# Computing x by tokens on halves of the array's rows, four chunks in one run, and dividing strip 0's output products at other places

## The chip, the cores and the metric

One core of a Trainium2 chip. The metric is the device time of one execution in microseconds (us). Executions of one kernel agree within about 0.3%. Traces show when each instruction started, to a few nanoseconds.

Engines are named as in the profile: PE is TensorE's matrix products, PEld its weight loads, DVE is VectorE, ACT is ScalarE, POOL is GpSimd, SP the queue that issues most DMAs. PSUM is the buffer in which products land; the kernel uses it as eight banks of 512 columns. A product's weights are its stationary operand; the other operand is streamed past them. The kernel can use the array whole, or as two halves of its columns or of its rows: that is called its tiling here.

## The reference, cut to what matters

```python
# q, k, v: (batch 8, heads 8, tokens 576, dim 64), inputs float32
kv  = einsum('bhsd,bhse->bhde', k, v)                  # 64 x 64 a head
o   = einsum('bhsd,bhde->bhse', q, kv)
x   = o / sqrt(mean(o*o, -1) + 1e-6) * g_norm          # -> (4608 tokens, 512)
out = ((x @ w_a) * (x @ w_b)) @ w_out                  # d_ff = 1536
```

## The kernel before

The second half dominates. Tokens go in nine strips of 512. In a strip, each of 12 column blocks of d_ff is one unit: four products with `w_a` into one PSUM bank, four with `w_b` into another, ACT copies the first (`asb`), DVE multiplies the two (`ab`). Then come four token blocks of 12 output products each. These products are 128x512 and run on the whole array.

The attention of batches 2 to 7 is woven into strips 1 to 6. x is computed by tokens there, in five chunks a batch: q (transposed, two heads in 128 rows) is the stationary operand, and a block-diagonal `kvb` of two heads is streamed. ACT squares, DVE sums, ACT takes the reciprocal root, POOL applies `g_norm`, DVE multiplies, and a transposing DMA puts x into `xt`.

```python
# banks: products a and b rotate over AB, x takes 5 + c % 3, k-by-v sits in 7
AB = (4, 1, 2, 0)
...
def tx(self, c, i):                       # one chunk of 128 tokens
    t0, r = self.rows(c)
    for p in range(NP):                   # 4 pairs of heads
        nc.tensor.matmul(P[:, i, p * 128 : (p + 1) * 128],
                         lhsT=self.qT[:, p, t0 : t0 + 128],
                         rhs=kvb[self.b % 2][:, p, :], start=True, stop=True)
    nc.scalar.activation(sqt[c % 3][r], self.by_head(i)[r], AF.Square)
```

In strip 0 the attention of batch 1 is woven into the output products instead. After token block 0 come six pieces of six products, into one bank only, `O = 3`. The other banks hold attention; bank 6 (`SS`) does so only from the third piece on.

```python
h1, h2 = range(0, FC // 2), range(FC // 2, FC)          # FC = 12
...
pieces = [(1, h1), (1, h2), (2, h1), (2, h2), (3, h1), (3, h2)]
for n, (g, fcs) in enumerate(pieces):
    halves = 0 < n < NP
    o_mm(0, g, O, fcs, halves=halves)                   # 6 products of block g
    if fcs is h2:
        o_out(0, g, O)                                  # DVE or ACT empties bank 3
    if 0 <= n - 2 < NP:
        A.pss(n - 2, SS, halves=halves)                 # sums of squares, banks 6 and 7
        A.pst(n - 2, X[n % 2])
    if 0 <= n - 1 < NP:
        A.x(n - 1, X[(n - 1) % 2], halves)
        A.psq(n - 1, X[(n - 1) % 2])
    if n < NP:
        A.qtr(n, 2)                                     # transposes of q
        A.kv1(n, 2)                                     # k-by-v product, waits for k and v
        A.kv_out(n, P[:, 2, STRIP - D :])
        A.qtr_out(n, 2)
```

## Time and profile before

| | before |
|---|---|
| time, median of the first three runs | 315.73 us |
| span of the profiled run | 313.8 us |
| PE busy | 98% of the span |
| PE's waits on others | 1.2 us and 0.4 us |
| matrix products in the trace | 1935 |

The first lines of the page (busy time, share of the span, instructions), the clock by slices, and the groups of products:

```profile
PE 308.6 (98%) x1935; PEld 149.0 (47%) x1935; DVE 141.5 (45%) x235; ACT 115.9 (37%) x225; POOL 101.2 (32%) x123
...
PEclk9999999999999999999999999999999999999999
...
L321 PE MATMUL P<-xt,wa_t 128*128 128x512 bf16 x432 | 111.9, 380 | 0.0
...
L271 PE MATMUL P<-kvb,qT 128*128 128x128 bf16 x120 | 11.6, 220 | 0.0
```

All waits of PE on other engines, before (who waited, on what: total us, times, longest):

```profile
PE P L407 <- DVE eps_t L424: 1.2, 1, 1.2
PE P L156 <- ACT sq L220: 0.4, 1, 0.4
```

PE is the limit, at full clock. But its ends are modelled (a 128x512 product is shown as 0.38 us long), so a gap of up to 0.17 us can hide in a "busy" PE. The sound reading is the distance from one start to the next. In this trace it is 0.216 us between 128x512 products from 50 us to the end, with few exceptions. The timeline of PE in strip 2 shows the exceptions (start us, us, engine, line, operation, shapes, count):

```profile
87.62 1.03 PE L321 MATMUL P<-xt,wb_t 128*128 128x512 bf16 x4
88.58 0.82 PE L173 MATMUL P<-vtl,ktl 128*64 128x64 bf16 x40
89.33 1.04 PE L321 MATMUL P<-xt,wa_t 128*128 128x512 bf16 x4
90.21 1.03 PE L321 MATMUL P<-xt,wb_t 128*128 128x512 bf16 x4
...
91.93 0.39 PE L271 MATMUL P<-kvb,qT 128*128 128x128 bf16 x4
92.16 1.03 PE L321 MATMUL P<-xt,wb_t 128*128 128x512 bf16 x4
```

Four products with one of the weights take 0.86 us, 4 x 0.216 (those from 89.33 to 90.21, the first after a run, 0.01 longer). A chunk of x (L271) takes 0.223 us (91.933 to 92.156) and costs nothing beyond its own array time. The k-by-v run (L173), which works on halves of the array's columns, is different: from 87.62 to 88.58 is 0.96 us where four products take 0.86. That is the first part of what a change of tiling costs.

In strip 0 the timeline of PE shows the weave of output products (L156 with `wo_t`), transposes (L197) and k-by-v (L173):

```profile
39.23 0.45 PE L197 MATMUL P<-ident,qt 96*64 96x96 bf16 x12
39.79 0.38 PE L173 MATMUL P<-vt,kt 96*64 96x64 bf16 x12
39.97 1.49 PE L156 MATMUL P<-wo_t,ab 128*64 128x512 bf16 x12
...
41.52 0.45 PE L197 MATMUL P<-ident,qt 96*64 96x96 bf16 x12
42.01 0.38 PE L173 MATMUL P<-vt,kt 96*64 96x64 bf16 x12
42.19 1.49 PE L156 MATMUL P<-wo_t,ab 128*64 128x512 bf16 x12
```

Twelve transposes take 0.26 us undisturbed; here 0.56 us pass from 39.23 to 39.79, and 0.49 from 41.52 to 42.01. In both places the k-by-v product starts 0.04 us after its v has landed (39.74 and 41.96 in the trace). These are holes, though the list of waits does not show them. The twelve instructions from 39.97 are the second half of token block 1.

### The profile page before, as it was taken

Reading aid. Unit: us, or ns where it says so; the run is one execution under the profiler, and the core shown is the slowest. Engines: PE = TensorE matmul, PEld = TensorE weight load, DVE = VectorE, ACT = ScalarE, POOL = GpSimd, SP = SyncE. Lnnn points to the kernel's source line nnn. Section 1 sums busy time; section 2 is a strip of 40 time slices with the busy share of each in tenths; the row PEclk is TensorE's granted clock in tenths of the full one; section 3 lists DMA queues with packets and bytes.
Section 4 is the critical chain, followed back from the end, with each engine's and each line's share of the span. In section 5 each row is a group of like instructions: output and inputs, shape, how many; then the busy total and the mean of one; then the engine's idle time right before and its main releaser. Section 6 shows DMA issues by size and latency. Waiting matters only on the chain.

```text
span 313.8 us, 5034 instructions
## 1 busy us (share of the span) xinstructions
PE 308.6 (98%) x1935; PEld 149.0 (47%) x1935; DVE 141.5 (45%) x235; ACT 115.9 (37%) x225; POOL 101.2 (32%) x123
## 2 busy tenths in 40 slices
PE   8999999999999999999999999999999999999995
PEld 3544474454445444544454445544544444444443
DVE  4544335356337703583377123761683134214321
ACT  3643155453246313551464024622651233123310
POOL 8954891282453730139038200320230000000000
PEclk9999999999999999999999999999999999999999
DMA  8999999999799799059988980073022200030002
GB/s 182 197 196 199 201 183 160 229 146 157 172 171 166 103 197 154 2 95 139 207 125 116 169 175 2 17 159 111 1 50 60 102 0 0 36 100 1 0 36 100
DMA packets 94253, 36.19 MB, mean 115 GB/s; under 512 B 64918, under 2 KB 89750, under 8 KB 94230
## 3 DMA queue, kind: packets, MB, share of 16 engines
q0 software_dynamic: 59120, 18.44, 53.8%
q1 hardware_dynamic: 34642, 16.87, 23.3%
q10 hardware_dynamic: 468, 0.57, 0.6%
q8 instruction: 15, 0.25, 0.3%
q14 instruction: 8, 0.07, 0.1%
HBM read 37.78 MB, written 12.98 MB: 162 GB/s over the span
## 4 chain that ended last, share of the span: by engine, by line
PE 86%; DMA 7%; POOL 4%; issue 1%; ACT 0%; POOLq 0%
PE P L321 53%; PE P L156 29%; DMA wb_t<-in_moe_w_b_dram 6%; PE P L271 2%; PE P L173 2%; DMA vt<-in_v_dram 2%; POOL qt L116 1%; POOL wo_t L131 1%; POOL kt L116 1%; POOL vt L116 1%; POOL wa_t L441 0%; POOL wb_t L441 0%; PE P L197 0%; POOL wa_t L127 0%; ACT o_end L619 0%
## 5 line engine op out<-in xcount | busy, mean ns | idle before, releaser
L339 DVE TENSOR_TENSOR ab<-P,asb 128x512 bf16<-128x512 f32 x108 | 74.5, 691 | 103.5 <-PE P L321 87.0
L321 PE MATMUL P<-xt,wa_t 128*128 128x512 bf16 x432 | 111.9, 380 | 0.0
L321 PE MATMUL P<-xt,wb_t 128*128 128x512 bf16 x432 | 111.8, 379 | 0.0
L335 ACT CAST asb<-P 128x512 bf16<-128x512 f32 x108 | 63.0, 585 | 92.4 <-PE P L321 92.4
L156 PE MATMUL P<-wo_t,ab 128*128 128x512 bf16 (+2 forms) x462 | 95.8, 374 | 0.0
L156 PEld LDWEIGHTS <-ab 128*128 128x128 bf16 (+1 forms) x462 | 43.7, 99 | 48.0
L321 PEld LDWEIGHTS <-wa_t 128*128 128x128 bf16 x432 | 41.4, 98 | 47.4 <-issue 0.2
L321 PEld LDWEIGHTS <-wb_t 128*128 128x128 bf16 x432 | 41.5, 98 | 47.0 <-DMA wb_t<-in_moe_w_b_dram 0.2
L294 POOL TENSOR_TENSOR sqt<-rst,g_all 128x512 f32<-128x512 f32 (+1 forms) x24 | 25.0, 1043 | 96.2 <-ACT rst L287 96.2
L392 ACT COPY osb<-P 128x512 f32<-128x512 f32 x17 | 9.9, 585 | 67.5 <-PE P L156 62.2
L394 DVE COPY osb<-P 128x512 f32<-128x512 f32 x18 | 12.4, 691 | 44.0 <-PE P L156 39.5
L139 POOL DMA_DIRECT2D qs<-in_q_dram x12 | 19.8, 1653 | 0.7 <-issue 0.3
L282 DVE TENSOR_REDUCE sst<-sqt 128x8 f32<-128x512 f32 (+1 forms) x24 | 16.3, 680 | 1.9 <-ACT sqt L278 1.4
L303 DVE TENSOR_TENSOR qv<-P,sqt 128x512 bf16<-128x512 f32 (+1 forms) x24 | 16.5, 686 | 0.3
L278 ACT ACTIVATE sqt<-P 128x512 f32<-128x512 f32 (+1 forms) x24 | 14.4, 599 | 4.2 <-PE P L271 4.1
L271 PEld LDWEIGHTS <-qT 128*128 128x128 bf16 x120 | 9.2, 98 | 7.1
L271 PE MATMUL P<-kvb,qT 128*128 128x128 bf16 x120 | 11.6, 220 | 0.0
L287 ACT ACTIVATE rst<-sst,eps_t 128x8 f32<-128x8 f32 (+1 forms) x30 | 9.0, 300 | 4.6 <-DVE sst L282 4.3
L238 DVE SCALAR_TENSOR_TENSOR xt<-P,g_col,rs 128x288 bf16<-128x288 f32 x16 | 7.5, 512 | 5.2 <-ACT rs L228 5.2
L294 POOL TENSOR_TENSOR k_x<-rst,g_all 128x512 f32<-128x512 f32 x6 | 6.3, 1042 | 8.8 <-ACT rst L287 8.8
L131 POOL DMA_DIRECT2D wo_t<-in_moe_w_out_dram x12 | 6.4, 530 | 6.7 <-DMA wb_t<-in_moe_w_b_dram 3.2
L184 ACT CAST kvb<-P 64x64 bf16<-64x64 f32 (+1 forms) x16 | 4.6, 285 | 10.5 <-PE P L173 10.4
(67 smaller groups left out, 123.1 us busy)
## 6 DMA issues: line engine op xcount, KB each, us to landing
out_dram<-osb SPq DMA_DIRECT2D x23, 256.0 KB, 2.1
qs<-in_q_dram POOLq DMA_DIRECT2D x12, 288.0 KB, 6.9
ktl<-in_k_dram POOLq DMA_DIRECT2D x6, 512.0 KB, 8.8
vtl<-in_v_dram POOLq DMA_DIRECT2D x6, 512.0 KB, 11.6
out_dram<-osb SPq DMA_DIRECT2D x13, 128.0 KB, 2.3
wo_t<-in_moe_w_out_dram POOLq DMA_DIRECT2D x12, 128.0 KB, 6.0
wa_t<-in_moe_w_a_dram POOLq DMA_DIRECT2D x5, 256.0 KB, 9.2
wb_t<-in_moe_w_b_dram POOLq DMA_DIRECT2D x5, 256.0 KB, 9.8
```

The source lines that it names most:

```text
L139: nc.gpsimd.dma_start(out=d[:, hs, :], in_=q[b, hs].rearrange("h t d -> t h d"))
L156: nc.tensor.matmul(o[r], lhsT=lhsT[:, r], rhs=rhs, **kw)
L271: nc.tensor.matmul(P[:, i, p * 128 : (p + 1) * 128], lhsT=self.qT[:, p, t0 : t0 + 128], rhs=kvb[self.b % 2][:, p, :], start=True, stop=True,)
L278: nc.scalar.activation(sqt[c % 3][r], self.by_head(i)[r], AF.Square)
L282: nc.vector.reduce_sum(sst[c % 3][r], sqt[c % 3][r], axis=mybir.AxisListType.X)
L294: nc.gpsimd.tensor_mul(sqt[c % 3][r], rst[c % 3][r].unsqueeze(2).to_broadcast([n, H, D]), g_all[r].unsqueeze(1).to_broadcast([n, H, D]),)
L303: nc.vector.tensor_mul(t[r], self.by_head(i)[r], sqt[c % 3][r])
L321: nc.tensor.matmul(self.a if w is wa_t else self.b, lhsT=w[:, kc, self.fc * 128 : (self.fc + 1) * 128], rhs=xt[:, kc, t0 : t0 + STRIP], st ...
L335: nc.scalar.copy(self.t, self.a)
L339: nc.vector.tensor_mul(abt[self.s % 2][self.fc], self.b, self.t)
L392: nc.scalar.copy(t, P[:, i, :])
L394: nc.vector.tensor_copy(t, P[:, i, :])
```

## The change

x is computed by four chunks in one run on halves of the rows: 64x128 weights (one head's q), 64 columns streamed, the lower-row head into banks 4 and 5 and the upper-row head into banks 6 and 7. The last chunk stays whole and comes later, in bank 4. Products a and b rotate over three banks. The k-by-v result is copied whole into `kvs`, and two ACT copies make the block-diagonal `kvb` for the last chunk. Strip 0's 36 output products are divided 8, 6, 6, 6, 5, 5 instead of six times 6.

```diff
+        def tx(self):
+            for c in range(LC):                          # LC = 4
+                t0, _ = self.rows(c)
+                for p in range(NP):
+                    for j, (i, c0) in enumerate(self.place(c)):   # banks 4 or 5, 6 or 7
+                        r = slice(j * D, (j + 1) * D)
+                        nc.tensor.matmul(P[:, i, c0 + p * D : c0 + (p + 1) * D],
+                            lhsT=self.qT[r, p, t0 : t0 + 128],
+                            rhs=self.kvs[r, p, :], start=True, stop=True)
...
-    pieces = [(1, h1), (1, h2), (2, h1), (2, h2), (3, h1), (3, h2)]
-    for n, (g, fcs) in enumerate(pieces):
+    cuts = (12, 20, 26, 32, 38, 43, 48)
+    for n, cut in enumerate(cuts[1:]):
         halves = 0 < n < NP
-        o_mm(0, g, O, fcs, halves=halves)
-        if fcs is h2:
-            o_out(0, g, O)
+        for i in range(cuts[n], cut):
+            g, fc = divmod(i, FC)
+            o_mm(0, g, O, (fc,), halves=halves)
+            if fc == FC - 1:
+                o_out(0, g, O)
...
-    n_ab[0] = 1
+    ab_banks[:] = [0, 1, 2]
```

More of the change, by code (lines that the diff above doesn't have):

```diff
@@ L78 @@
     k32 = k_x[0:EP].rearrange("p (h c d) -> p h c d", h=2, c=EC)
-    sqt = [sb([128, H, D], FP32, f"sqt{i}") for i in range(2)]
-    sqt.append(k_x[:, 0 : H * D].rearrange("p (h d) -> p h d", h=H))
+    sqt = [sb([128, 2, NP, D], FP32, f"sqt{i}") for i in range(2)]
+    sqt.append(k_x[:, 0 : H * D].rearrange("p (j h d) -> p j h d", j=2, h=NP))
     sst = [sb([128, H], FP32, f"sst{i}") for i in range(3)]
@@ L179, in kv, with kv_out @@
                     )
-        def kv_out(self, ps, src, copy=nc.scalar.copy):
+        def kv_out(self, ps, src):
             for j in range(2):
                 r = slice(j * D, (j + 1) * D)
-                copy(kvb[self.b % 2][r, ps, r], src[r])
+                nc.scalar.copy(kvb[self.b % 2][r, ps, r], src[r])
         def kv1(self, p, i):
@@ L263, in rows, with place, by_head, tx_last @@
             return t0, slice(c * 128 - t0, 128)
-        def by_head(self, i):
-            return P[:, i, :].rearrange("t (h d) -> t h d", h=H)
-        def tx(self, c, i):
-            t0, r = self.rows(c)
+        def place(self, c):
+            return tuple((4 + 2 * j + c // 2, c % 2 * (STRIP // 2)) for j in range(2))
+        def by_head(self, c):
+            if c == LC:
+                return P[:, 4, :].rearrange("t (p j d) -> t j p d", j=2, p=NP)
+            (i, c0), (j, _) = self.place(c)
+            o = P[:, i : j + 1 : j - i, c0 : c0 + STRIP // 2]
+            return o.rearrange("t j (p d) -> t j p d", p=NP)
+        def tx(self):
[4 more added lines that the diff above has]
+                        r = slice(j * D, (j + 1) * D)
+                        nc.tensor.matmul(
+                            P[:, i, c0 + p * D : c0 + (p + 1) * D],
+                            lhsT=self.qT[r, p, t0 : t0 + 128],
+                            rhs=self.kvs[r, p, :],
+                            start=True,
+                            stop=True,
+                        )
+        def tx_last(self):
             for p in range(NP):
                 nc.tensor.matmul(
-                    P[:, i, p * 128 : (p + 1) * 128],
-                    lhsT=self.qT[:, p, t0 : t0 + 128],
+                    P[:, 4, p * 128 : (p + 1) * 128],
+                    lhsT=self.qT[:, p, S - 128 : S],
                     rhs=kvb[self.b % 2][:, p, :],
@@ L277, in tx, with tsq @@
                 )
-            nc.scalar.activation(sqt[c % 3][r], self.by_head(i)[r], AF.Square)
+        def tsq(self, c):
+            _, r = self.rows(c)
+            nc.scalar.activation(sqt[c % 3][r], self.by_head(c)[r], AF.Square)
         def tss(self, c):
             _, r = self.rows(c)
-            nc.vector.reduce_sum(sst[c % 3][r], sqt[c % 3][r], axis=mybir.AxisListType.X)
+            nc.vector.reduce_sum(
+                sst[c % 3][r],
+                sqt[c % 3][r].rearrange("t j p d -> t (j p) d"),
+                axis=mybir.AxisListType.X,
+            )
         def trs(self, c):
@@ L294, in trs @@
             nc.gpsimd.tensor_mul(
-                sqt[c % 3][r],
+                sqt[c % 3][r].rearrange("t j p d -> t (j p) d"),
                 rst[c % 3][r].unsqueeze(2).to_broadcast([n, H, D]),
@@ L298, in trs, with txt @@
             )
-        def txt(self, c, i):
+        def txt(self, c):
             t0, r = self.rows(c)
             t = x_tok[c // 3][:, c % 3]
-            nc.vector.tensor_mul(t[r], self.by_head(i)[r], sqt[c % 3][r])
+            nc.vector.tensor_mul(
+                t[r].rearrange("t (p j) d -> t j p d", j=2), self.by_head(c)[r], sqt[c % 3][r]
+            )
             t0 += self.b * S
@@ L343, in rest @@
             self.part_b(kcs)
-    AB = (4, 1, 2, 0)
-    n_ab = [0]
+    ab_banks = [4, 1, 2, 0]
     def ab_bank():
-        n_ab[0] += 1
-        return AB[(n_ab[0] - 1) % len(AB)]
+        ab_banks.append(ab_banks.pop(0))
+        return ab_banks[-1]
     def ffn_ab(s, fc, between=None):
@@ L523 @@
     u3.part_b()
-    n_ab[0] = 0
     for fc in range(4, FC):
@@ L529 @@
     A = Attn(1)
-    h1, h2 = range(0, FC // 2), range(FC // 2, FC)
     nc.sync.dma_start(out=gate_d, in_=vt[1][0:1, H - 1, EC - 1, D - 1 : D])
@@ L570, in slot @@
             xs = tuple(x0 + x for x in (0, 1.5, 2.5, 4, 5))
+        k0, x0 = {1: (5, 6.5), 2: (1, 2.5), 3: (4, 5.5), 4: (0, 0.5), 5: (4, 5.5), 6: (0, 0.5)}[s]
         if n == k0 and s in (1, 2, 3, 5):
@@ L577, in slot @@
             for i, a in enumerate(two):
-                a.kv_out(slice(0, NP), kb[:, i], nc.vector.tensor_copy if i else nc.scalar.copy)
-        for c, x in enumerate(xs):
-            i = 5 + c % 3
-            if n == x:
-                A.tx(c, i)
-            elif n == x + 0.5:
+                (nc.scalar.copy if i else nc.vector.tensor_copy)(a.kvs, kb[:, i])
+        m = n - x0
+        if m == 0:
+            A.tx()
+        if m == 1:
+            A.kv_out(slice(0, NP), A.kvs)
+        if m == 5:
+            A.tx_last()
+        for c in range(LC + 1):
+            if m == 1.5 * c:
+                A.tsq(c)
+            if m == (1, 2, 4, 5, 7)[c]:
                 A.tss(c)
-            elif n == x + 1:
+            if m == (1, 2, 4, 5, 7)[c] + 0.5:
                 A.trs(c)
-            elif n == x + 2.5:
-                A.txt(c, i)
+            if m == (1, 2, 4, 5, 7)[c] + 1.5:
+                A.txt(c)
     for s in range(1, N_STRIP - 1):
```

## The prediction

> **What bounds the kernel now.** TensorE. The page gives PE 98% busy at granted clock 1.0; the list of waits shows PE waiting 1.2 us (start) and 0.4 us. Busy time is modelled, so I read start-to-start distances in the timeline of PE: from 50 us to the end every 128x512 matmul follows the last after 0.216 us; DVE (45%), ACT (37%) and POOL are hidden. Only instructions taken from PE's stream, or gaps in it, are worth time.
>
> **x by tokens, before.** A chunk is 4 whole-array matmuls, 56 ns apart: 0.223 us (timeline: 64.06 to 64.28), no entry cost. 24 of 30 chunks change: 24 x 0.223 = 5.4 us, 1.7% of the time, is all that could be won. Each batch's last chunk is unchanged.
>
> **After.** Per batch 32 matmuls of 64 rows by 128 columns, 64 wide: 16 pairs on halves of the rows, into different banks. The nearest thing in this trace is the k-by-v product (halves of the columns, also 64 wide): 40 matmuls take 0.75 us, a pair each 32 ns. It also prices a change of tiling: the matmul before the run is followed after 0.309 instead of 0.216 us, the first pair takes 20 ns more, the last matmul 0.1 us more: about 0.22 us a run. The Trainium skill, "TensorEngine Tiling (Array Packing)", Key Properties, says that changing the mode drains TensorE; this trace agrees with those 0.22 us.
> Per batch: 0.22 + 16 x 0.032 = 0.74 us against 0.89: 0.95 us saved over six batches. The open term is the pair: its weight loads have 128 columns, not 64. The skill, "TensorE: Matmul & The Clock Gate", Part 3, says loads overlap running matmuls where the row group differs; this trace has no row-only pairs. At 56 ns a pair the part loses 1.35 us; break-even is 42 ns.
>
> **Banks.** x holds 4 to 7, so a and b rotate over three banks instead of four. A bank must be free 1.73 us after its product ended; 0.17 us of drain, a 0.585 (ACT) or 0.69 us (DVE) eviction and 0.1 us of signalling leave 0.8 us. One foreign DVE instruction (0.68 us) ahead fits, two don't; one or two short stretches per batch come near. I expect 0 to 0.3 us in all. The extra ACT copies are hidden.
>
> **Strip 0.** In the timeline the k-by-v product of pair 0 starts at 39.79, just after its v landed at 39.74: 0.28 us of PE idle; pair 1 at 42.01 (v at 41.96): 0.22 us. The first piece of 8 instead of 6 matmuls fills the first hole, and most of the second closes with it. About 0.35 us saved.
>
> **Sum:** 315.73 - 0.95 - 0.35 + 0.2 = 314.6; with some weight on slower pairs, 314.7 us. Range 313.9 to 316.9. Chances: faster by over 2%: 0.01, within 2%: 0.97, slower: 0.02.
>
> **What would show the steps.** Timeline of PE: the run of 32 lasts 0.6 to 0.75 us to the next product's start (pair 32 ns) or 1.0 (56 ns); products a in strips 1 to 7 keep 0.863 us (no bank stall), and the list of waits names no asb or ab as PE's releaser; strip 0's first k-by-v run follows its transposes without the 0.28 us hole.
>
> **What would make it wrong.** Weight loads of row halves that don't overlap (+1 to +5 us); repeated bank stalls where DVE serves x; a transpose of x landing after strip 2 begins.

## The result, and the profile after

| | before | after |
|---|---|---|
| time, median of 6 runs each | 315.67 us | 316.19 us |
| ratio, 95% interval | | 1.0012 (0.9999 to 1.0025) |
| span of the profiled run | 313.8 us | 314.5 us |

Ratios here are the mean time of one kernel's fast runs over that of the other's of the same rounds, so not quite the ratio of the medians quoted.

The predicted range held, but the predicted number (314.7) did not come: about 1.5 us are missing. The page after, the same lines (line numbers differ between the kernels: L321 is L355 after, L271 is L285 for the run and L296 for the last chunk):

```profile
PE 305.1 (97%) x1997; PEld 146.1 (46%) x2031; DVE 140.9 (45%) x235; ACT 117.9 (38%) x231; POOL 101.2 (32%) x123
...
PEclk9999999999999999999999999999999999999999
...
L355 PE MATMUL P<-xt,wa_t 128*128 128x512 bf16 x415 | 109.5, 379 | 0.7 <-issue 0.2
```

PE's busy time fell by 3.5 us and the span grew. Some of that fall is no saving: this trace lacks 34 of its 2031 matmul records (1997 stand beside PEld's 2031; `xt,wa_t` has 415 of 432), and so are waits put down to "issue", like the last line of the next view, which stand at such places. All waits of PE, after:

```profile
PE P L156 <- DVE osb L427: 1.2, 1, 1.2
PE P L440 <- DVE eps_t L457: 1.2, 1, 1.2
PE P L156 <- ACT osb L425: 0.7, 1, 0.7
PE P L156 <- ACT sq L220: 0.4, 1, 0.4
...
PE P L355 <- issue: 0.2, 1, 0.2
```

There are two new waits of PE, both of output products (L156) on `osb`, the copy out of bank 3. Neither is in strips 1 to 7. There the new x run looks so:

```profile
65.19 1.03 PE L355 MATMUL P<-xt,wa_t 128*128 128x512 bf16 x4
66.15 0.64 PE L285 MATMUL P<-kvs,qT 64*128 64x64 bf16 x32
66.72 1.04 PE L355 MATMUL P<-xt,wb_t 128*128 128x512 bf16 x4
67.59 0.38 PE L355 MATMUL P<-xt,wa_t 128*128 128x512 bf16 x1
```

The four products before the run (65.19) are followed after 0.96 instead of 0.86 us, and the run of 32 takes 0.57 us. The starts inside it (from the records, not in this merged view) alternate 3 and 26 ns apart: a pair each 29 ns. The x part works better than I had costed it.

And strip 0, all engines, with PEld and POOL left out; compare the L156 groups with those of before:

```profile
39.83 0.45 PE L197 MATMUL P<-ident,qt 96*64 96x96 bf16 x12
...
40.11 0.35 PE L173 MATMUL P<-vt,kt 96*64 96x64 bf16 x12
...
40.30 1.03 PE L156 MATMUL P<-wo_t,ab 128*64 128x512 bf16 x8
40.51 0.42 ACT L184 CAST kvb<-P 64x64 bf16<-64x64 f32 x2 [5.16 <-PE P L173]
...
40.96 0.46 DVE L204 COPY qT<-P 128x576 bf16<-128x576 bf16 x1 [2.06 <-ACT kvb L184]
41.37 0.58 ACT L425 COPY osb<-P 128x512 f32<-128x512 f32 x1 [0.44 <-PE P L156]
...
42.01 0.62 PE L156 MATMUL P<-wo_t,ab 128*64 128x512 bf16 x4 [0.68 <-ACT osb L425]
...
42.44 0.44 PE L156 MATMUL P<-qT,kvb 128*64 128x288 bf16 x4
...
45.36 1.06 PE L156 MATMUL P<-wo_t,ab 128*64 128x512 bf16 x8
...
45.67 0.94 DVE L238 SCALAR_TENSOR_TENSOR xt<-P,g_col,rs 128x288 bf16<-128x288 f32 x2 [1.30 <-ACT rs L228]
...
46.53 0.45 DVE L204 COPY qT<-P 128x576 bf16<-128x576 bf16 x1
...
46.90 0.68 DVE L427 COPY osb<-P 128x512 f32<-128x512 f32 x1
...
47.64 0.62 PE L156 MATMUL P<-wo_t,ab 128*64 128x512 bf16 x4 [1.22 <-DVE osb L427]
```

The first hole is gone: k-by-v (40.11) follows its transposes (39.83) after 0.28 us. But then block 1 ends after 4 of the piece's 6 products (8 instructions, as each is two halves), block 2 must start in the same bank, and PE stands still until ACT has copied it (41.37 to 41.95; PE goes on at 42.01). The second time the copy is DVE's, behind DVE's own work for x and a copy of qT (46.53): it starts only at 46.90, and PE goes on at 47.64.

To sum up the two parts, I split each trace at the first product of strip 1 (the first output product starts at 35.26 us before and 35.42 after, strip 1 at 50.25 and 52.24):

| trace | first output product of strip 0 to first product of strip 1 | from there to the end |
|---|---|---|
| before | 14.99 us | 263.54 us |
| after | 16.82 us | 262.25 us |

If each change acts only in its own stretch, x on row halves saved 1.29 us (right column) and the new division cost 1.83 us (left); experiments 1 and 2 test that. (The rest of the difference in span, 0.16 us, lies in the start-up before strip 0's outputs, which moves by 0.22 and 0.46 us between the traces of one kernel in experiments 1 and 7.)

### The profile page after: what moved, and what is told of

Read it like the earlier page. It is cut to its first block, busy times and chain, and to the rows that moved or that the text cites. A ratio compares the mean times of both kernels' runs of the same rounds, so it can differ in the third digit from the quotient of the medians.

```text
span 314.5 us, 5181 instructions
## 1 busy us (share of the span) xinstructions
PE 305.1 (97%) x1997; PEld 146.1 (46%) x2031; DVE 140.9 (45%) x235; ACT 117.9 (38%) x231; POOL 101.2 (32%) x123
## 4 chain that ended last, share of the span: by engine, by line
PE 95%; DVE 1%; ACT 1%; issue 1%; DVEq 0%
PE P L355 59%; PE P L156 30%; PE P L440 2%; PE P L173 2%; PE P L285 1%; PE P L197 1%; PE P L211 0%; ACT rs L228 0%; DVE ab L373 0%; PE P L296 0%; ACT sq L220 0%; DVE xt L238 0%; DVE qT L204 0%; DVE osb L427 0%; ACT osb L425 0%
## 5 line engine op out<-in xcount | busy, mean ns | idle before, releaser
L355 PE MATMUL P<-xt,wb_t 128*128 128x512 bf16 x425 | 110.9, 379 | 0.5
L355 PE MATMUL P<-xt,wa_t 128*128 128x512 bf16 x415 | 109.5, 379 | 0.7 <-issue 0.2
L156 PE MATMUL P<-wo_t,ab 128*128 128x512 bf16 (+2 forms) x453 | 95.5, 373 | 2.5 <-DVE osb L427 1.2
L156 PEld LDWEIGHTS <-ab 128*128 128x128 bf16 (+1 forms) x462 | 43.6, 99 | 50.6 <-issue 2.5
L355 PEld LDWEIGHTS <-wa_t 128*128 128x128 bf16 x432 | 41.9, 98 | 49.9 <-issue 0.2
L355 PEld LDWEIGHTS <-wb_t 128*128 128x128 bf16 x432 | 41.6, 98 | 48.7 <-DMA wb_t<-in_moe_w_b_dram 0.2
L440 PE MATMUL P<-zeros 128*128 128x512 bf16 x16 | 6.8, 578 | 1.2 <-DVE eps_t L457 1.2
L228 ACT ACTIVATE rs<-P,eps_t 128x576 f32<-128x576 f32 (+1 forms) x9 | 6.1, 688 | 4.9 <-PE P L156 4.6
L204 DVE COPY qT<-P 128x576 bf16<-128x576 bf16 x8 | 3.6, 456 | 6.4 <-ACT kvb L184 4.6
```

Source lines behind the costliest of these rows:

```text
L156: nc.tensor.matmul(o[r], lhsT=lhsT[:, r], rhs=rhs, **kw)
L355: nc.tensor.matmul(self.a if w is wa_t else self.b, lhsT=w[:, kc, self.fc * 128 : (self.fc + 1) * 128], rhs=xt[:, kc, t0 : t0 + STRIP], st ...
L440: nc.tensor.matmul(P[:, i, 0:cols], lhsT=zeros[:, 0:128], rhs=zeros[:, 0:cols], start=True, stop=True)
```

## The experiments

Two theories of the missing time. Mine, from the traces: the division costs 1.6 us (from the two waits; the split says 1.83) because two blocks end inside a piece. The rivals: the three banks, the extra copies or the tiling changes in strips 1 to 6 eat the gain; or the gaps in strip 0 come from landing data. All kernels were correct.

### 1. The changed kernel with the old division

```diff
-    cuts = (12, 20, 26, 32, 38, 43, 48)
+    cuts = (12, 18, 24, 30, 36, 42, 48)
```

> The changed kernel with strip 0's outputs divided as before (12, 18, 24, 30, 36, 42, 48). Theory: the row-half runs save 1.3 us (24 x 0.2235 us less 6 x 0.68 us) and the new division costs 1.6 us, because two token blocks now end inside a piece and the next block must wait for the only output bank (PE gaps of 0.84 and 1.42 us). So here about 314.4 us, 0.9960 of before, and no PE gap over 0.3 us between 35 and 52 us. Rival: the loss comes with the three banks, the extra ACT copies or the changes of tiling in strips 1 to 6, and the division is neutral or saves 0.35 us as I predicted: then 316.2 to 316.5 us.

Measured: 314.28 us, ratio to before 0.9959 (0.9945 to 0.9973). The trace split: 15.12 and 262.26 us. The waits on `osb` are gone, and the hole before the first k-by-v product is back, this time with its name in the timeline:

```profile
39.26 0.45 PE L197 MATMUL P<-ident,qt 96*64 96x96 bf16 x12
39.88 0.38 PE L173 MATMUL P<-vt,kt 96*64 96x64 bf16 x12 [0.18 <-DMA vt<-in_v_dram]
40.07 1.49 PE L156 MATMUL P<-wo_t,ab 128*64 128x512 bf16 x12
```

(That hole is 0.34 us; I had expected none over 0.3.) The theory's number came. That of the rivals in strips 1 to 6 did not: the banks, copies and tiling changes are all still in this kernel.

### 2. The kernel before with the new division alone

> The kernel before with the new division of strip 0's outputs alone. Theory: two waits for the output bank, 0.84 and 1.42 us, less the closed holes of some 0.6 us: +1.6 us, about 317.3 us, 1.005 of before. Rival (my prediction): the division fills the holes before the k-by-v products and saves 0.35 us: 315.3 us, 0.999.

The edit is the `cuts` part of the diff above, on the kernel before. Measured: 317.63 us, 1.0066 (1.0053 to 1.0078), that is +2.1 us where 1.6 were expected. The split: 16.82 and 263.52 us. So the loss in strip 0 is the same 1.83 us with and without the x part, and the two parts add up. My 1.6 left out a third, smaller wait that the shorter last pieces open: with five products instead of six before it, the last pair's x comes 0.22 us too early for the copy of qT (L204) that it needs. The waits of PE name the same two copies:

```profile
PE P L156 <- DVE osb L394: 1.2, 1, 1.2
...
PE P L156 <- ACT osb L392: 0.7, 1, 0.7
```

### 3. The changed kernel, block 1 of strip 0 in a bank of its own

```diff
-            o_mm(0, g, O, (fc,), halves=halves)
+            o_mm(0, g, SS if g == 1 else O, (fc,), halves=halves)
             if fc == FC - 1:
-                o_out(0, g, O)
+                o_out(0, g, SS if g == 1 else O)
```

> The changed kernel with the second token block of strip 0 summed in bank 6, which is idle until then, so that the third block does not wait for bank 3. If the wait for the bank is the cause, the first gap (0.84 us, at about 41.2 us) goes and the second (1.42 us) stays: 315.35 us, 0.9973 of the changed kernel's time. If the gaps come from something else at that place (the landing of k or v, the change of tiling inside a piece), nothing goes: 316.2 us.

Measured: 315.44 us, 0.9996 (0.9983 to 1.0008) of before. Expected were 315.35 us. The split: 16.01 and 262.25 us, so strip 0 lost 0.81 us of its cost. The place where PE stood still at 41.2 us is closed, and the second is as it was:

```profile
39.92 1.47 PE L156 MATMUL P<-wo_t,ab 128*64 128x512 bf16 x12
41.22 0.41 PE L156 MATMUL P<-qT,kvb 128*64 128x288 bf16 x4
...
44.21 1.06 PE L156 MATMUL P<-wo_t,ab 128*64 128x512 bf16 x8
46.45 0.62 PE L156 MATMUL P<-wo_t,ab 128*64 128x512 bf16 x4 [1.19 <-DVE osb L427]
```

Here the 12 instructions from 39.92 run through in 1.30 us; after, the same 12 took 2.14 (40.30 to 42.44). Only the bank was changed. This shows that the first wait was for the bank. No run moves the second wait alone; it is named by the list of waits, and it is gone in experiments 1 and 7, where block 2 ends with a piece.

### 4. and 5. In which order the halves come

> The changed kernel with each chunk's four products of the lower half of the rows first, then the four of the upper half, in place of alternating. Theory: two neighbours run at once only on different rows, so that most of the products follow at about 29 ns each in place of 29 ns a pair: a run takes about 0.95 us in place of 0.57, +2.3 us over six runs, about 318.4 us, 1.007 of the changed kernel. Rival: the array overlaps them whatever their order (the gain is only the halved width): 316.2 us and an unchanged run of 0.57 us.

```diff
-                for p in range(NP):
-                    for j, (i, c0) in enumerate(self.place(c)):
+                for j, (i, c0) in enumerate(self.place(c)):
+                    for p in range(NP):
```

Measured: 316.37 us, 1.0028 of before; the changed kernel was at 1.0012 in its own rounds, and the intervals overlap. A run took 0.59 us instead of 0.57. My expectation failed. It was also badly worked out: even in strict order the two neighbours at each boundary between groups may overlap, which makes some 22 ns a product, not 29 (an estimate: three distances of 29 ns and one of 3). But the records show about 15 ns a product. So I asked with larger groups:

> The changed kernel with all 16 products of the lower rows of a batch first, then all 16 of the upper. In groups of four the order did not matter (run of 0.587 in place of 0.573 us). Two readings: (a) the array looks ahead over a few instructions and starts a product of the idle half early, so that the halves still run at once; with 16 in a group it can't, starts are 27 to 29 ns apart, a run takes 0.9 to 1.0 us, +2.4 us over six runs, 1.0075 of the changed kernel; (b) a half alone takes a product of 64 columns every 14.5 ns, whatever the other half does: the run stays at 0.59 us and the time at that of the changed kernel.

The edit puts the loop over `j` outermost. Measured: 318.34 us, 1.0090 (1.0076 to 1.0104), +2.2 us on the changed kernel by medians of different rounds; the split agrees (16.82 and 264.43 us, +2.18 in the right column). The timeline of PE around the run, first with groups of four, then with groups of 16:

```profile
66.16 0.65 PE L285 MATMUL P<-kvs,qT 64*128 64x64 bf16 x32
66.75 1.04 PE L355 MATMUL P<-xt,wb_t 128*128 128x512 bf16 x4
```

```profile
65.95 1.01 PE L286 MATMUL P<-kvs,qT 64*128 64x64 bf16 x32
66.89 1.04 PE L356 MATMUL P<-xt,wb_t 128*128 128x512 bf16 x4
```

0.59 against 0.94 us. In the run of 16 and 16 the starts are 29 ns apart, except about the middle, where some eight come 8 to 21 ns apart; then 29 ns again. This rules out reading (b) and fits (a): halves run at once where products of the other half stand a few instructions ahead, and not farther. It also shows that the gain of the change is the two halves running at once: without that a run costs 0.94 + 0.11 us, more than the 0.89 us of before. Most records do not say which half a start belongs to, but one does. With groups of four, the built program lets one product of the run raise PE's semaphore: the 28th in order, the last of the lower half. In the trace the product with that mark is the 31st to start, in all six runs. (In the changed kernel it is the 31st in both.) So three products of the upper half, which stand behind it, started before it. With groups of 16 the short distances begin after the 13th start, with three products of the lower half left: three again, but that one is inferred from the distances.

### 6. The kernel before on three banks

```diff
-    n_ab[0] = 1
+    n_ab[0] = 0
+    AB[:] = [0, 1, 2]
```

> The kernel before with products a and b from strip 1 on rotating over three banks (0, 1, 2) in place of four; nothing else. Theory: the evictions keep up and it costs nothing: 1.000 of before, within 0.0015, and no a or b product lengthened in the trace. Rival: with one foreign VectorE instruction ahead a bank comes free too late, and PE stalls in some units where x is made: +0.5 us or more, 1.0015 or more.

Measured: 315.47 us, 0.9996 (0.9982 to 1.0010). No a or b product is lengthened in the trace except where k-by-v changes the tiling. The three-bank rotation is free here. With the new x runs beside it the same shows in the two complete traces of experiment 7 with the old division (2031 records): from strip 1 on no distance from an a or b product to the next start is over 0.23 us but those before the four k-by-v and six x runs (0.31). I had allowed up to 0.3 us for it.

### 7. A version meant to beat both, and its comparison

```diff
-    cuts = (12, 20, 26, 32, 38, 43, 48)
+    cuts = (12, 20, 26, 31, 36, 42, 48)
```

with block 1 in bank 6 as in experiment 3.

> A version meant to beat both: row-half runs, block 1 of strip 0 in bank 6, and pieces cut at 20, 26, 31, 36, 42: the hole before the first k-by-v product is filled, no block ends inside a piece with its successor waiting for the same bank. Theory: 0.2 to 0.4 us below the changed kernel with the old division, about 314.0 us, 0.995 of before. If the old division's holes before k-by-v are bound by the landing of v and only move, it equals the old division: 0.996.

> The changed kernel with the old division of strip 0 again, on the same chip as the version meant to be best: 0.996 of before as in its first run.

Measured: 314.04 us, 0.9958 (0.9945 to 0.9970), against 314.18 us, 0.9960 (0.9947 to 0.9972) with the old division. Against the trace of experiment 1 the new one looked 0.43 us shorter in strip 0 (0.12 us against the trace of its own rounds), but started 0.46 us later: its list of waits has one of 0.5 us for a landing of `wb_t`. So I ran both again.

> The version meant to be best, again. In its first trace the stretch from the first output product of strip 0 to the first product of strip 1 was 14.69 us against 15.12 us with the old division, but its start lay 0.46 us later, and the times did not tell the two apart. If the later start was chance, this run shows the stretch at 14.7 us again and a median 0.2 to 0.4 us below the old division's; if it is a part of the version, the medians agree again within 0.15 us.

> The changed kernel with the old division beside it, for the same comparison: stretch 15.1 us, 0.996 of before.

Measured: 314.09 us, 0.9964 (0.9950 to 0.9977), against 314.20 us, 0.9961 (0.9947 to 0.9975). Strip 0's stretch was 14.69 and 14.84 us with the new division, and 15.12, 14.81 and 14.99 us with the old. A gain of 0.1 to 0.2 us is not resolved. The traces show why so little comes: in the second trace of the new division the hole before the first k-by-v product is filled, but the next three still start 0.04 us after their v has landed (41.98, 44.24 and 46.42 against 41.94, 44.20 and 46.38), so most of the hole only moves. With the old division the first hole was 0.34, 0.09 and 0.27 us in the three traces, as v landed. The old division is as good, and simpler. Both beat the kernel before by 0.4%, or 1.1 to 1.4 us by the medians.

## Why the prediction was right or wrong

- **The range held; the number did not.** Predicted 314.7 us (313.9 to 316.9), measured 316.19 us. "Within 2%" came. That the change would gain a microsecond was wrong. The range held because it was wide, from 1.8 us gained to 1.2 us lost, and because an unforeseen loss in strip 0 was partly covered by x and the banks doing better than predicted: that is luck, and speaks for no step.
- **x on row halves: right in mechanism, and a little too small.** Predicted 0.95 us, measured 1.29 us (the right column of the split, and experiment 1). A pair took 29 ns instead of the 32 borrowed from the column halves. The two weight loads of 128 columns, the open term, did not hinder it: they last 92 to 96 ns each in the records, no longer than the 98 ns of the whole-array loads, and they overlap running products, with groups of 16 (experiments 4 and 5) even those of the same half (95 ns a load, starts 29 ns apart). The change of tiling cost 0.21 us a run, as estimated (0.22): 0.095 before it, 0.01 after it, and 573 - 16 x 29.3 = 104 ns inside.
- **Banks: right.** Estimated 0 to 0.3 us, measured nothing (experiment 6).
- **Strip 0: the step that failed.** "The first piece of 8 instead of 6 matmuls fills the first hole, and most of the second closes with it. About 0.35 us saved." The holes did close, 0.27 and 0.23 us by the starts in the trace, and a wait of 0.13 us with them; but behind the first hole PE was already late from the wait for the bank, and experiment 7 gained at most 0.1 to 0.2 us where no such wait stood. But I looked only at the places where a piece ends, not at where a block ends. With 8, 6, 6, 6, 5, 5 products, blocks 1 and 2 end inside a piece. Before, transposes, k-by-v and x stood between a block's last product and the next block's first, and hid the copy out of the one output bank. Now the next product follows at once, and PE waits 0.84 and 1.41 us; a third wait of 0.22 us opens before the last x. 0.84 + 1.41 + 0.22 - 0.63 = 1.84 us, the 1.83 us of the split: predicted 0.35 us saved, measured 1.83 us lost. I had worked out the reuse of banks with care for a and b, where it cost nothing, and never for bank 3, where it cost everything.
- **What would have shown it in advance:** the built order of PE's instructions has the products of block 2 directly behind those of block 1, into the same bank, with a wait for ACT before the first (the second time, for DVE). The duration of that copy (0.585 us on ACT, 0.69 on DVE) was in the trace, and so was the 0.17 us by which a product's recorded end lies behind the start of the next.

## What to carry to other kernels

When you move the cuts of a woven stream, list for each PSUM bank what stands on PE between the last product into it and the first of its next use; if less stands there than the end of the last product, the copy and the copying engine's queue take together, PE stops, as it did here for 0.84 and 1.41 us. Two changes handed over together can cancel; splitting the trace at a point between them tells each one's share without another run, and the best version was one of them alone. In this kernel products of 64 rows and 64 columns were worth pairing on row halves: a pair took 29 ns instead of 56, so that some eight pairs pay the 0.21 us for the change of tiling (an estimate), with the halves no more than a few instructions apart.

## What the Trainium skill lacked or had wrong

- "TensorEngine Tiling (Array Packing)", Key Properties, says that changing the tiling mode drains TensorE and gives no price. Here it is 0.21 us a run in all: 0.095 us before the run, 0.104 us inside it, 0.01 us after it.
- "TensorE: Matmul & The Clock Gate", Part 3, says that matmuls are in strict program order, and only weight loads are pulled ahead. With groups of four products on the same half of the rows a strict order of starts would give about 22 ns a product (an estimate from the 29 ns of one half), and the trace shows about 15; with groups of 16 it shows 29 ns but for about eight products at the boundary. And with groups of four the product marked by a semaphore is 28th in the program and 31st to start, in six of six runs: products of an idle row half did start ahead of waiting ones of the other, past three of them.
- The same part gives speedups for row tiling at 512 columns, none for short products that alternate on two halves of the rows with new weights each time. Here a pair of 64 columns took 29 ns, weight loads of 128 columns included.
- "PSUM — Partial Sum Buffer", in its summary of rules, advises to evacuate promptly, without a figure for what a bank that is still full costs the next products. Here the first product after a block in the same bank started 0.84 us (ACT's copy, at once) and 1.41 us (DVE's, behind other work) later than it would have without the wait; experiment 3 shows the first to be the bank's.
